# Attention and MLP on one core: another order of a pair's steps, with roundings moved to GpSimd

## The chip, the cores and the metric

The kernel runs on one core of a Trainium2 chip. The metric is the device time of one execution in microseconds (us); smaller is better. The engines are PE (matrix products and transposes), DVE (VectorE), ACT (ScalarE), POOL (GpSimd) and SP, whose queue issues the DMAs. Each engine works through its own queue in the order in which the program was written; engines wait for each other through semaphores.

## What is computed

Attention with a bias that depends on the distance of two positions, then an MLP with an ELU. Everything is float32.

```
B, H, S, D = 4, 8, 576, 64
scores = q @ k^T / sqrt(D) + bias          # bias: 8 heads x 576 x 576, a small net of log1p|i-j| / log1p(i)
attn   = exp(scores - rowmax);  attn /= attn.sum(-1) + 1e-9
x      = (attn @ v) as 2304 tokens x 512
g      = elu(x @ w_in)                     # 512 -> 2048
out    = g @ w_out                         # 2048 -> 512
```

## The kernel before

There are three stages: the bias tables (to about 50 us), attention (to 275 us), and the MLP. The change is in attention and its hand-over to the MLP.

**Pairs.** Attention works on 16 pairs: a pair `n` is two heads (e = 0, 1) of one batch, four pairs a batch. The 576 queries of a pair are four blocks of 128 rows (u = 0..3, two heads each) and a tail of 64 rows, in which both heads share one block (u = 4). For a block the steps are, by the letters used in the lists:

- `S`: scores on PE (line 361), three products of a high and a low part for each half of the keys. A block's two heads take the two score tiles `ps0`, `ps1`; the tail takes one.
- `X`: on DVE, bias added, row minimum of the negated scores (line 388), which frees the score tile; then on ACT the exponential with its row sum (line 400); after head 1 a GpSimd copy `md` of the last 64 key columns of both heads (line 403).
- `T`: transposes on PE of the exponentials into two of three banks `w` (line 474; the tail's, `T4`, at 483 to 487). `M` transposes the `md` tiles: with two digits into spare columns of a score tile (line 458), with one digit into a `w` bank (line 443).
- `P`, `Q`: copies of the transposed tiles from PSUM to the tiles `pta`, `ptb` (lines 495 to 501, and 446, 462). The letter at the end says the engine, A for ACT, V for DVE.
- `V`: products with the values on PE (line 517), half 0 from `pta`, half 1 from `ptb`, five key chunks each. `C` copies the sum out (line 523); there is one bank `v`, so a half's first product waits for the `C` of the half ahead of it.

**Weights.** Between these steps stands the decoding of one of 16 weight tiles a pair, whose raw words come by one 1 MB DMA into a single tile `raw` (line 330): `scale` (POOL, line 335), `low` (DVE, line 339), `sign` (DVE, line 343, after which the next `raw` is loaded), `shift` (DVE, line 345, then an integer add on POOL, line 348), and the store by SP.

**Split of q and k.** `high` rounds the next pair's q and k to fp32r (four casts, line 139), `rest` subtracts (four subtractions on POOL, line 143).

**The lists.** `STEPS` is a table of five lines, written out by hand. A pair's turn runs through the five lines; a step that begins with `a` is of this pair, with `y` of the pair before it, so that the two overlap. `step` walks a line and emits its steps, so the list sets the order on every engine's queue. `FIRST` serves pair 0, `SECOND` pair 1, `LATE` (alike `STEPS`) the last four, `LAST` what is left after pair 15. After each line, `aside` issues loads, the store of a weight tile, and `pad_v`; `flush` issues the attention output's stores. `early` holds work for the MLP, by pair and place: loads of the MLP's input (`load_x`: x and its row factors rr), its scaling (`scale_x`), and the parts of `B11` to `B22` (`high_x`, `low_x`); `one` and `two` in a list are the places for those that run on DVE, in pairs 6, 7, 10 and 12 to 15.

**The sums' inverses.** After each four pairs the row sums are lifted by 1e-9 (POOL, line 415), inverted (DVE, line 411), transposed (`turn`), copied (`turned`) and stored.

Of the kernel before, what the change touches and what calls it, by code (L numbers as in the profile page):

```python
# [10 lines left out]
F32 = mybir.dt.float32  # L11
# [13 lines left out]
def kernel(  # L25
# [517 lines left out]
    PRODS = (("A11", "B11"), ("S2", "T2"), ("A12", "B21"), ("S3", "T3"), ("S1", "T1"), ("A22", "T4"), ("S4", "B22"))  # L543


    def load_x(j, r, h, part=None):
        t0 = (2 * j + h) * HB
        c0 = KH * r
        if not part:
            if h == 0:  # L550
                xr[j, r] = keep.tile([P, KH, 2, HB], F32, tag=f"xr{r}", name=f"xr{r}", bufs=1)
            st["rr", j, r, h] = keep.tile([P, KH, HB], F32, tag="rr", name="rr", bufs=1)
        x, rr = xr[j, r][:, :, h], st["rr", j, r, h]
        M = NCH * P
        done = 0
        while done < HB:
            b, s = divmod(t0 + done, S)
            m = min(HB - done, S - s)
            if part in (None, min(done, 1)):
                nc.sync.dma_start(out=x[:, :, done:done + m], in_=xd[b][:, c0:c0 + KH, s:s + m])  # L560
                rows = rd[b].rearrange("(h u) t -> h (u t)", h=HP)[c0:c0 + KH]
                cuts = [(0, s, m, s)]
                if s < M:
                    cuts.append((1, s, min(m, M - s), M + P + s))
                if s + m > M:
                    k = max(s, M)
# [60 lines left out]
    def attention():  # L627
# [14 lines left out]
        )  # L642
        FIRST = (
            "aS0 aS4 aX00 aX01 high rest aX40",
# [2 lines left out]
            "aS3 aT1 w3 aP10A aX30 aX31",  # L647
            "zS0 aT4 aP11V aP40A aP41A",
        )
        SECOND = (  # L650
            STEPS[0].replace("low ", "").replace("aX00", "aX00 scale").replace("aX01", "aX01 low"),
            *STEPS[1:],
        )
        LATE = (
# [5 lines left out]
        )  # L660
        LAST = (
            "yT2 yP20A yP21V yV00 yV01 yV02 low yM0 yV03 yQ0A",
            "yT3 yP30A yP31V yV04 sign yC0V shift yM1 yQ1A",
            "yV10 yV11 yV12 yV13 yV14 yC1A",
        )
        late = []

        V, G = nc.vector, nc.gpsimd
        early = {
            (5, 0): [(load_x, 0, 0, 0)],  # L670
            (6, "one"): [(scale_x, 0, 0, 0, V)],
            (6, 0): [(load_x, 0, 1, 0)],
            (7, "one"): [(scale_x, 0, 1, 0, V)],
            (8, 0): [(load_x, 0, 0, 1, 0)],
            (9, 0): [(load_x, 0, 0, 1, 1)],
            (10, "one"): [(scale_x, 0, 0, 1, V)],
# [26 lines left out]
        def step(N, line):  # L703
            for tok in line.split():
# [21 lines left out]
                if k == "S":  # L726
# [4 lines left out]
                        ]  # L731
                    if ("ps", n, i[0]) not in st:
                        scores(n, i[0], first_bank if (n, i[0]) == (0, 1) else pair_bank)
                    if i[0] == NCH and n % HP == 0 and n > 0:
                        turn(n // HP - 1, (n, NCH))
                elif k == "X":
                    expo(n, *i)
                    if i[0] == NCH and n % HP == 0 and n > 0:
                        late.extend(turned())
                elif k == "T":  # L740
                    trans_p(n, i[0])
                elif k == "P":
# [31 lines left out]
        def aside(n, i):  # L774
            if i == 4:
                weights(n - 1, "store")
            if i == 0 and n > 0:
                load_v(n)
                pad_v(n - 1)
            if i == 2:  # L780
                if 0 < n < NP - 2:
                    load_pair(n + 2)
            if n == 0 and i == 1:
                open_banks()
            if n > 0 and n % HP == 0:
                if i == 0:
                    lift(n // HP - 1)
                if i == 1:
                    invert(n // HP - 1)
            others(n, i)  # L790
            if n < NP - 1:
                return
            if i == 0:
                load_w(0)
                load_w(1)
            if i == 2:
                high_w(0)
            if i == 3:
                low_w(0, nc.vector)
            if i == 4:  # L800
                load_w(2)

        for n in range(NP):
            for i, line in enumerate(FIRST if n == 0 else SECOND if n == 1 else STEPS if n < NP - 4 else LATE):
                flush()
                step(n, line)
                aside(n, i)
# [371 lines left out]
```

## Time and profile before

| what | value |
| --- | --- |
| time, median of 3 runs | 660.24 us (659.71 to 660.47) |
| the profiled execution: its time | 660.98 us |
| its span | 659.2 us |
| PE busy, share of the span | 650.7 us, 99% |
| DVE, ACT, POOL busy | 477.5, 449.9, 144.3 us |
| chain that ended last, by engine | PE 87%, ACT 6%, DMA 4% |

The span is what the profiler saw between the first and the last instruction; 1.8 us lie around it. A busy share is an average over three stages with different limits; in attention one pair's turn takes about 13.4 us and is read by itself below. PE's starts are recorded and its ends are modelled, so distances from start to start are used for PE.

### The profile page before, as it was taken

How to read it: one execution, taken by the hardware profiler on the slowest of the kernel's cores; microseconds unless marked ns; L12 is line 12 of the kernel's file. 1: busy time of each engine (PE TensorE's matmuls, PEld its weight loads, DVE VectorE, ACT ScalarE, POOL GpSimd, SP SyncE). 2: the span in 40 equal slices, each digit the busy share in tenths (PEclk: the TensorE clock that was granted, in tenths of full speed). 3: DMA queues.
4: the chain of work that ended last, by engine and by line, in shares of the span. 5: the costliest groups of instructions: out<-in, count | busy, mean ns of one | idle time of the engine just before them, and what ended most of it. 6: DMA issues, size and time to landing. Idle time of an engine off the chain costs nothing.

```text
span 659.2 us, 14081 instructions
## 1 busy us (share of the span) xinstructions
PE 650.7 (99%) x5334; PEld 524.5 (80%) x5334; DVE 477.5 (72%) x992; ACT 449.9 (68%) x984; POOL 144.3 (22%) x207
## 2 busy tenths in 40 slices
PE   8999999999999999999999999999999999999997
PEld 5446767767677677799998889899899899899896
DVE  6998888888888998886778998554466554444444
ACT  7998999989999999775666676544345544444443
POOL 1003566655665667600000000000000000000000
PEclk9999999999999999999999999999999999999999
DMA  6998667786877666456798678976854465444102
GB/s 171 221 230 236 213 226 216 200 270 208 243 240 242 192 206 226 145 178 230 254 329 316 241 255 334 382 254 241 284 207 191 198 253 229 191 176 175 65 1 95
DMA packets 47427, 144.42 MB, mean 219 GB/s; under 512 B 9968, under 2 KB 22912, under 8 KB 39680
## 3 DMA queue, kind: packets, MB, share of 16 engines
q1 hardware_dynamic: 45872, 141.01, 64.7%
q10 hardware_dynamic: 1488, 2.52, 1.1%
q8 instruction: 42, 0.69, 0.4%
q14 instruction: 25, 0.20, 0.1%
HBM read 91.92 MB, written 40.97 MB: 202 GB/s over the span
## 4 chain that ended last, share of the span: by engine, by line
PE 87%; ACT 6%; DMA 4%; DVE 1%; issue 1%; SPq 1%; DVEq 0%; ACTq 0%
PE acc L919 30%; PE h L972 27%; PE wv L517 12%; PE ps L361 10%; PE wt L474 5%; ACT rel L241 3%; ACT bo L264 2%; DMA bias<-bo 2%; DMA raw<-in_wd_dram 2%; PE wm L443 1%; DMA T<-in_rtab_dram 1%; PE acc L972 1%; PE wt L483 1%; ACT ss L400 1%; DMA out_dram<-os 0%
## 5 line engine op out<-in xcount | busy, mean ns | idle before, releaser
L919 PE MATMUL acc<-wB,gh 128*128 128x512 f32 x528 | 171.3, 392 | 0.0
L972 PE MATMUL h<-bias 128*128 128x384 f32 x552 | 111.5, 338 | 0.0
L919 PEld LDWEIGHTS acc<-wB,gh 128*128 128x128 f32 x528 | 98.1, 188 | 14.3
L388 DVE CUSTOM_DVE_ANT_0 ss<-ps,bias 128x576 f32<-128x576 f32 x128 | 91.8, 755 | 21.2 <-PE ps L361 11.3
L972 PEld LDWEIGHTS h<-bias 128*128 128x128 f32 x552 | 99.9, 188 | 7.5 <-DVE rs L430 0.4
L919 PE MATMUL acc<-wB,gl 128*128 128x512 f32 x264 | 103.8, 393 | 0.0
L400 ACT ACTIVATE ss<-ss,nm 128x576 f32<-128x576 f32 x128 | 99.3, 779 | 6.4 <-DVE nm L388 6.0
L952 ACT CAST gh<-e 128x384 fp32r<-128x384 f32 x96 | 49.3, 514 | 40.4 <-DVE e L951 39.6
L957 ACT ACTIVATE e<-c 128x384 f32<-128x384 f32 x66 | 34.7, 525 | 53.5 <-DVE c L1003 53.4
L946 DVE TENSOR_TENSOR gl<-e,gh 128x384 fp32r<-128x384 f32 x96 | 53.2, 554 | 19.0 <-ACT gh L952 16.6
L957 ACT ACTIVATE e<-h 128x384 f32<-128x384 f32 x28 | 13.8, 491 | 68.8 <-PE h L972 68.8
L951 DVE SCALAR_TENSOR_TENSOR e<-e,c 128x384 f32<-128x384 f32 x66 | 36.8, 557 | 30.6 <-ACT e L958 30.5
L972 PE MATMUL h<-bias,wA 128*128 128x384 f32 x276 | 56.3, 338 | 0.0
L919 PEld LDWEIGHTS acc<-wB,gl 128*128 128x128 f32 x264 | 49.5, 187 | 7.8
L972 PEld LDWEIGHTS h<-bias,wA 128*128 128x128 f32 x276 | 50.2, 188 | 3.8
L958 ACT ACTIVATE e<-e 128x384 f32<-128x384 f32 x96 | 50.5, 526 | 3.0
L1003 DVE TENSOR_TENSOR c<-h,u 128x384 f32<-128x384 f32 x66 | 36.7, 556 | 20.1 <-PE h L972 20.1
L474 PEld LDWEIGHTS wt<-ident,ss 64*128 64x128 f32 x1024 | 39.2, 139 | 11.7 <-issue 6.9
L251 PE MATMUL bps<-rel,cs 128*32 128x288 f32 x576 | 47.3, 413 | 0.8 <-ACT bo L264 0.4
L361 PE MATMUL ps<-kh,qh 64*128 64x288 f32 x256 | 45.9, 341 | 1.4 <-ACT pta L462 1.4
L403 POOL TENSOR_SCALAR md<-ss 128x128 f32<-128x128 f32 x64 | 21.2, 331 | 116.5 <-ACT ss L400 112.7
L474 PE MATMUL wt<-ident,ss 64*128 64x64 f32 x1024 | 45.8, 227 | 0.8 <-DVE nm L388 0.4
(145 smaller groups left out, 1217.3 us busy)
## 6 DMA issues: line engine op xcount, KB each, us to landing
wB<-wB SPq DMA_DIRECT2D x22, 1024.0 KB, 6.5
raw<-in_wd_dram SPq DMA_DIRECT2D x16, 1024.0 KB, 5.9
bias<-wA SPq DMA_DIRECT2D x9, 1792.0 KB, 8.9
wA<-wA SPq DMA_DIRECT2D x8, 1792.0 KB, 8.6
wa<-wf SPq DMA_DIRECT2D x20, 512.0 KB, 4.8
wA<-bias SPq DMA_DIRECT2D x5, 1792.0 KB, 9.9
wf<-da SPq DMA_DIRECT2D x16, 512.0 KB, 3.5
bias<-bo SPq DMA_DIRECT2D x17, 288.0 KB, 6.5
```

The source lines that it names most:

```text
L251: nc.tensor.matmul(ps[32 * g:32 * g + 32, f, 0:HS], lhsT=W2, rhs=rel[g][:, f * HS:(f + 1) * HS], start=True, stop=True,)
L361: nc.tensor.matmul(ps[:, f, 0:HS], lhsT=(qh, ql)[q][r, u * P:(u + 1) * P] if u < NCH else qd[n % 2][q], rhs=k[r, f * HS:(f + 1) * HS], sta ...
L388: nc.vector.tensor_tensor_reduce(out=s.rearrange("p (f x) -> p f x", f=2), in0=st["ps", n, u][e][:, :, 0:HS], in1=bap.rearrange("p (f x) - ...
L400: nc.scalar.activation(s, s, AF.Exp, bias=nm, scale=-1.0, accum_out=st["sm", b][:, hp, col:col + 1])
L474: nc.tensor.transpose(banks[r][:, x * TAIL:(x + 1) * TAIL], ss[q, c:c + P], ident[q, q])
L517: nc.tensor.matmul(st["pv", n, half][e * D:(e + 1) * D, 0:N], lhsT=l, rhs=r, start=start, stop=stop)
L919: nc.tensor.matmul(acc[j, t], lhsT=x[:, t * P:(t + 1) * P], rhs=w, start=(count[j, t] == 1), stop=(count[j, t] == 6 * NQ),)
L946: nc.vector.tensor_sub(gl, t, gh.bitcast(F32))
L952: nc.scalar.copy(g[i, e][0][:, h * HB:(h + 1) * HB], t)
L957: nc.scalar.activation(t, src, AF.Relu, scale=-1.0)
L958: nc.scalar.activation(t, t, AF.Exp, scale=-1.0)
L972: nc.tensor.matmul(ps, lhsT=a[f][c], rhs=x[y][c], start=(start and k == 0), stop=(stop and k == len(todo) - 1), skip_group_check=not start,)
```

## The change

The table `STEPS` is written anew. The tail's scores stand second (S0, S4, S1, S2, S3) where they stood third; transposes stand behind the values and ahead of a set of scores more often; `low` and `sign` stand around the second exponential, `shift` in the last line. On the copies: the middle half `Q1` goes from DVE to ACT, `C0` and the tail's two copies `P40`, `P41` from ACT to DVE. The roundings `high` become `highG`, on GpSimd. `SECOND` is `STEPS`, so pair 1's `scale` is issued at `low`. Pair 15 has a list of its own (`FINAL`), and `LAST` is in another order. `load_x` can issue x alone or rr alone; the first two loads of x go two pairs and one pair ahead of their rr. `scale_x` of the second goes from pair 7 to pair 8. The transpose of the sums stands behind the third set of scores of a pair, whichever that is; lift and inversion stand behind the first two exponentials.

```
 STEPS = (
-    "aS0 yM0a0 yT3 yQ01A yV02 one low aX00 yQ00A yP30A aX01 yV01 yV03",
-    ...
-    "aS3 aT4 aP11V yV13 aP40A aP41A yV11 aX30 yV12 aX31 yC1A",
+    "aS0 yM0a0 yT3 yV02 yQ00A yQ01A yP31A aX00 yM1",
+    ...
+    "aS3 aP00A shift aP01A aX30 yV10 yV12 yV11 aX31 yC1A aT4 aP41V aP40V",
 )
-SECOND = (STEPS[0].replace("low ", "").replace("aX00", "aX00 scale").replace("aX01", "aX01 low"), *STEPS[1:])
+SECOND = STEPS
+FINAL = (
+    ...
+    "aS2 rest yC0V aT1 one aP10A aX20 aP11V yV14 yV13 aX21 shift aT0 aP00A",
+    "aS3 yV10 aP01A aX30 aT4 yV12 yV11 aP40V aX31 aP41V yC1A",
+)
 early = {
-    (5, 0): [(load_x, 0, 0, 0)],
+    (3, 0): [(load_x, 0, 0, 0, None, "x")],
+    (5, 0): [(load_x, 0, 0, 0, None, "r")],
     (6, "one"): [(scale_x, 0, 0, 0, V)],
-    (6, 0): [(load_x, 0, 1, 0)],
-    (7, "one"): [(scale_x, 0, 1, 0, V)],
+    (6, 0): [(load_x, 0, 1, 0, None, "x")],
+    (7, 0): [(load_x, 0, 1, 0, None, "r")],
+    (8, "one"): [(scale_x, 0, 1, 0, V)],
...
-    if i[0] == NCH and n % HP == 0 and n > 0:
-        turn(n // HP - 1, (n, NCH))
+    if n % HP == 0 and n > 0:
+        st["nth"] = st.get("nth", 0) % (NCH + 1) + 1
+        if st["nth"] == 3:
+            turn(n // HP - 1, (n, i[0]))
...
-    for i, line in enumerate(FIRST if n == 0 else SECOND if n == 1 else STEPS if n < NP - 4 else LATE):
+    for i, line in enumerate(FIRST if n == 0 else SECOND if n == 1 else FINAL if n == NP - 1 else STEPS):
```

On PE, from the spare transposes behind S0 (line 458) on: T3 is line 474, values are line 517, the tail's scores are the rows with `qd`, the other scores those with `qh`. Before:

```order
L458 MATMUL ps<-ident,md 128x64 x4
L474 MATMUL wt<-ident,ss 128x64 x16
L517 MATMUL wv<-pta,vv 64x320 x6
L361 MATMUL ps<-kh,qh 128x288 x2
L361 MATMUL ps<-kl,qh 128x288 x2
L361 MATMUL ps<-kh,ql 128x288 x2
L361 MATMUL ps<-kh,qh 128x288 x2
L361 MATMUL ps<-kl,qh 128x288 x2
L361 MATMUL ps<-kh,ql 128x288 x2
L474 MATMUL wt<-ident,ss 128x64 x16
L517 MATMUL wv<-pta,vv 64x320 x2
```

The same place on PE after the change:

```order
L458 MATMUL ps<-ident,md 128x64 x4
L474 MATMUL wt<-ident,ss 128x64 x16
L517 MATMUL wv<-pta,vv 64x320 x2
L443 MATMUL wm<-ident,md 128x128 x2
L361 MATMUL ps<-kh,qd_108 128x288
L361 MATMUL ps<-kl,qd_108 128x288
L361 MATMUL ps<-kh,qd_109 128x288
L361 MATMUL ps<-kh,qd_108 128x288
L361 MATMUL ps<-kl,qd_108 128x288
L361 MATMUL ps<-kh,qd_109 128x288
L517 MATMUL wv<-pta,vv 64x320 x2
L474 MATMUL wt<-ident,ss 128x64 x16
```

One key chunk of values stands where three stood, the tail's scores follow S0 in place of S1's, and T2 stands behind values (ahead of S1) where it stood behind S1.

On POOL, one pair, from its `vz` (pad of the values' tail) to the next. Before, with `da` the weights' scale (335) and add (348):

```order
L154 TENSOR_SCALAR vz_114<-vv 64x64 x2
L348 TENSOR_TENSOR da<-da,dm 128x1024
L403 TENSOR_SCALAR md<-ss 128x128
L143 TENSOR_TENSOR kl<-kk,kh 128x576
L143 TENSOR_TENSOR ql<-qq,qh 128x512
L143 TENSOR_TENSOR qd_109<-qq,qd_108 64x64 x2
L403 TENSOR_SCALAR md<-ss 128x128 x2
L335 TENSOR_SCALAR da<-raw 128x1024
L403 TENSOR_SCALAR md<-ss 128x128
```

The same engine after the change:

```order
L154 TENSOR_SCALAR vz_114<-vv 64x64 x2
L335 TENSOR_SCALAR da<-raw 128x1024
L403 TENSOR_SCALAR md<-ss 128x128
L139 CAST qd_108<-qq 64x64 x2
L139 CAST qh<-qq 128x512
L139 CAST kh<-kk 128x576
L403 TENSOR_SCALAR md<-ss 128x128
L143 TENSOR_TENSOR kl<-kk,kh 128x576
L143 TENSOR_TENSOR ql<-qq,qh 128x512
L143 TENSOR_TENSOR qd_109<-qq,qd_108 64x64 x2
L403 TENSOR_SCALAR md<-ss 128x128
L348 TENSOR_TENSOR da<-da,dm 128x1024
```

The four casts of line 139 have come in, and the weights' add stands behind the subtractions, near the pair's end.

## Rows read from the trace of the kernel before

**Rows 1.** The page, its first section: busy us, share of span, instructions.
```profile
PE 650.7 (99%) x5334; PEld 524.5 (80%) x5334; DVE 477.5 (72%) x992; ACT 449.9 (68%) x984; POOL 144.3 (22%) x207
```

**Rows 2.** Busy time by stretch, a pair with `one` in it (pair 10).
```profile
core 0: us, PE busy (x) PEld busy (x) DVE busy (x) ACT busy (x) POOL busy (x), PEclk, DMA share, GB/s
185.50:199.00 13.50, 13.50 (x178) 9.71 (x176) 11.93 (x31) 12.72 (x36) 8.56 (x13) 1.00 0.73 228
```

**Rows 3.** Timeline of DVE: tail reduces of pairs 6, 7, 14, 15 (start, length).
```profile
139.81 0.76 DVE L388 CUSTOM_DVE_ANT_0 st<-ps,biast 128x576 f32<-128x576 f32 x1 [0.36 <-PE ps L361]
153.18 0.76 DVE L388 CUSTOM_DVE_ANT_0 st<-ps,biast 128x576 f32<-128x576 f32 x1 [0.36 <-PE ps L361]
...
247.29 0.76 DVE L388 CUSTOM_DVE_ANT_0 st<-ps,biast 128x576 f32<-128x576 f32 x1 [0.37 <-PE ps L361]
260.74 0.76 DVE L388 CUSTOM_DVE_ANT_0 st<-ps,biast 128x576 f32<-128x576 f32 x1 [0.37 <-PE ps L361]
```

**Rows 4.** Timeline of PE inside pair 10: start, length, line, count.
```profile
187.46 0.80 PE L474 MATMUL wt<-ident,ss 64*128 64x64 f32 x16
...
189.96 0.40 PE L361 MATMUL ps<-kh,qh 64*128 64x288 f32 x2
...
190.72 0.30 PE L361 MATMUL ps<-kh,ql 64*128 64x288 f32 x2
190.85 0.66 PE L474 MATMUL wt<-ident,ss 64*128 64x64 f32 x16
191.44 0.76 PE L517 MATMUL wv<-pta,vv 128*64 128x320 f32 x4
...
193.07 0.29 PE L361 MATMUL ps<-kh,qd 128*128 128x288 f32 x1
193.29 0.76 PE L517 MATMUL wv<-pta,vz 128*64 128x320 f32 x4
193.98 0.71 PE L474 MATMUL wt<-ident,ss 64*128 64x64 f32 x16
194.50 0.38 PE L361 MATMUL ps<-kh,qh 64*128 64x288 f32 x2
...
195.41 0.71 PE L474 MATMUL wt<-ident,ss 64*128 64x64 f32 x16
```

**Rows 5.** Pairs 5 and 6: the chain that ended last, then DVE's and PE's timeline.
```profile
123.90 9.97 DMA raw<-in_wd_dram
133.90 0.69 DVE L339 TENSOR_SCALAR dm<-raw 128x1024 int32<-128x1024 uint32 x1 [1.73 <-DMA raw<-in_wd_dram]
136.37 0.40 PE L361 MATMUL ps<-kh,qh 64*128 64x288 f32 x2 [1.41 <-ACT pta L462]
```

**Rows 6.** POOL's groups, whole span: busy us, mean ns of one, idle before.
```profile
L348 POOL TENSOR_TENSOR da<-da,dm 128x1024 int32<-128x1024 int32 x16 | 42.1, 2634 | 3.8 <-DVE da L345 2.5
L143 POOL TENSOR_TENSOR kl<-kk,kh 128x576 fp32r<-128x576 f32 x15 | 21.3, 1418 | 11.9 <-DVE kh L139 9.1 <-DMA kk<-in_k_dram 1.9 <-DMA raw<-in_wd_dram 0.8
L335 POOL TENSOR_SCALAR da<-raw 128x1024 f32<-128x1024 f32 x16 | 19.1, 1192 | 1.0 <-DMA raw<-in_wd_dram 0.9
L143 POOL TENSOR_TENSOR qd<-qq,qd 64x64 fp32r<-64x64 f32 x30 | 9.5, 317 | 1.1
L194 POOL COPY pick<-ident 128x128 f32<-128x128 f32 x1 | 0.3, 291 | 0.1
```

**Rows 7.** Hand-over to the MLP, timelines of POOL and DVE.
```profile
274.49 6.37 POOL L348 TENSOR_TENSOR da<-da,dm 128x1024 int32<-128x1024 int32 x1 [2.54 <-DVE da L345]
...
277.66 0.95 DVE L591 TENSOR_TENSOR T<-xr,xr 128x768 f32<-128x768 f32 x1
278.99 2.69 DVE L591 TENSOR_TENSOR T<-xr,T 128x768 f32<-128x768 f32 x1
```

**Rows 8.** DVE's and ACT's groups in pair 8; last a timeline row of DVE.
```profile
L343 DVE SCALAR_TENSOR_TENSOR dm<-raw,dm 128x1024 uint32<-128x1024 uint32 x1 | 1.2, 1220 | 0.0
L339 DVE TENSOR_SCALAR dm<-raw 128x1024 int32<-128x1024 uint32 x1 | 0.7, 690 | 0.0
L500 ACT COPY pta<-wt 128x256 f32<-128x256 f32 x2 | 0.7, 370 | 0.0
253.56 0.95 DVE L603 TENSOR_TENSOR bias<-xr,bias 128x768 fp32r<-128x768 f32 x1
```

More of the change, by code (lines that the diff above doesn't have):

```diff
@@ L543, with load_x @@
     PRODS = (("A11", "B11"), ("S2", "T2"), ("A12", "B21"), ("S3", "T3"), ("S1", "T1"), ("A22", "T4"), ("S4", "B22"))
-    def load_x(j, r, h, part=None):
+    def load_x(j, r, h, part=None, what="xr"):
         t0 = (2 * j + h) * HB
@@ L549, in load_x @@
         if not part:
-            if h == 0:
+            if h == 0 and "x" in what:
                 xr[j, r] = keep.tile([P, KH, 2, HB], F32, tag=f"xr{r}", name=f"xr{r}", bufs=1)
-            st["rr", j, r, h] = keep.tile([P, KH, HB], F32, tag="rr", name="rr", bufs=1)
-        x, rr = xr[j, r][:, :, h], st["rr", j, r, h]
+            if "r" in what:
+                st["rr", j, r, h] = keep.tile([P, KH, HB], F32, tag="rr", name="rr", bufs=1)
+        x, rr = xr[j, r][:, :, h], st.get(("rr", j, r, h))
         M = NCH * P
@@ L558, in load_x @@
             m = min(HB - done, S - s)
-            if part in (None, min(done, 1)):
+            if part in (None, min(done, 1)) and "x" in what:
                 nc.sync.dma_start(out=x[:, :, done:done + m], in_=xd[b][:, c0:c0 + KH, s:s + m])
+            if part in (None, min(done, 1)) and "r" in what:
                 rows = rd[b].rearrange("(h u) t -> h (u t)", h=HP)[c0:c0 + KH]
@@ L649, in attention @@
         )
-        SECOND = (
-            STEPS[0].replace("low ", "").replace("aX00", "aX00 scale").replace("aX01", "aX01 low"),
-            *STEPS[1:],
-        )
-        LATE = (
[5 rows of a table removed]
+        SECOND = STEPS
+        LATE = (
[5 rows of a table added]
+        )
+        FINAL = (
[5 rows of a table added]
         )
         LAST = (
-            "yT2 yP20A yP21V yV00 yV01 yV02 low yM0 yV03 yQ0A",
-            "yT3 yP30A yP31V yV04 sign yC0V shift yM1 yQ1A",
-            "yV10 yV11 yV12 yV13 yV14 yC1A",
+            "low yT2 yV00 yV01 yM0 yP21A yP20V yT3",
+            "yV02 yQ0A yP30A yV04 yV03 yP31A sign yV11 yM1 yC0V",
+            "yV13 yV12 shift yQ1A yV14 yV10 yC1A",
         )
@@ L733, in step @@
                         scores(n, i[0], first_bank if (n, i[0]) == (0, 1) else pair_bank)
-                    if i[0] == NCH and n % HP == 0 and n > 0:
-                        turn(n // HP - 1, (n, NCH))
+                    if n % HP == 0 and n > 0:
+                        st["nth"] = st.get("nth", 0) % (NCH + 1) + 1
+                        if st["nth"] == 3:
+                            turn(n // HP - 1, (n, i[0]))
                 elif k == "X":
                     expo(n, *i)
-                    if i[0] == NCH and n % HP == 0 and n > 0:
-                        late.extend(turned())
+                    if n % HP == 0 and n > 0:
+                        if i == [0, 0]:
+                            lift(n // HP - 1)
+                        if i == [0, 1]:
+                            invert(n // HP - 1)
+                        if "wr" in st and st["wr"][1] == (n, i[0]):
+                            late.extend(turned())
                 elif k == "T":
@@ L784, in aside @@
                 open_banks()
[L785 to L789, printed above, removed]
             others(n, i)
```

19 rows, old and new, of tables (FINAL, LATE, STEPS) are left out of this document.

## The prediction

> **What bounds the kernel now.** I read the page first: PE is busy for 99% of the span [rows 1], so the question is whether that busy time is work or only a modelled end. The busy time by stretch says for one pair in attention: PE 13.50 of 13.50 us, ACT 12.72, DVE 11.93, POOL 8.56 [rows 2]. ACT is near its limit too, so either could set the pace. The tail reduces give the pace: 13.37 us from pair 6 to pair 7 and 13.45 from pair 14 to 15 [rows 3]; the pairs from 12 on, which also carry work for the MLP, are the slower ones.
>
> PE's timeline inside pair 10 decides it [rows 4]. If PE waited for ACT or DVE, gaps between groups would differ from pair to pair. They repeat, and they follow the kind of neighbour: a set of 16 transposes starts values 0.59 us after its own start when it follows scores (190.85 to 191.44), and starts scores 0.52 us after its own start behind values (193.98 to 194.50). I see two places only where transposes run longer than their 0.66: T3 takes 0.80 and T1 0.71. T3 needs the second exponential of block 3, which on ACT stands behind the copies of the tail; that is a wait. So PE bounds attention before the change, with some 0.2 us a pair of real waiting. The MLP is a chain of PE instructions on both sides and isn't touched.
>
> One place stands out. In pair 6 the DVE waits 1.73 us for `raw` and PE then stands still for 1.41 us [rows 5]. That weight tile was asked for in pair 5 and landed 9.97 us later, since the load of x with its rr was issued just ahead of it on SP.
>
> **The change part by part.**
>
> *PE's order.* No product or transpose is added or dropped, so only the neighbours change. Scores followed by values start them 0.22 us after their last product (193.07 to 193.29), scores followed by transposes 0.13 (190.72 to 190.85) [rows 4]. S1 and S3 now have values behind them: +0.09 twice, +0.18. T2 and T4 stand ahead of scores in place of values: 0.52 for 0.59, -0.07 twice, -0.14. The copies of the tail leave ACT, so T3's wait should go: -0.14; T1's -0.05 likewise. The sum is -0.15 a pair. The bounds are 0 (both waits come back as others) and -0.3 (a set of scores behind transposes also starts quicker, which these rows don't settle). Pairs 1 to 5, 7, 9 and 11 have nothing else: 8 x -0.15 = -1.2 us.
>
> *Tail second.* S4 needs one score tile, so its products run while DVE still reduces block 0's second head. The ring of score tile, reduce, next scores gets shorter by about one tail's turn. As PE is the bound this buys slack and no time; I cost it at nothing, and what it must cover is the next point.
>
> *Copies between ACT and DVE.* The tail's copies are two of 0.37 us [rows 8] and two smaller ones; with C0 they go to DVE, and Q1 comes to ACT. DVE loses the four casts and gains these, about even. ACT gets about 1 us of air (an estimate: the two of 0.37, as much again for the smaller ones and C0, less Q1). Queued behind the tail's copies on DVE is the next pair's first reduce, and behind that S4 and S1; the copies fit into the time in which DVE would wait for S0's products, so nothing, with +0.3 a pair if they don't fit.
>
> *Roundings on GpSimd.* The trace has no cast on POOL. The nearest rows are the one-input copies: 291 ns for 128 columns and 1192 for 1024 [rows 6], about 1.0 ns a column. That makes 0.74 us for k (576), 0.68 for q (512) and 0.23 for each small one: 1.9 us a pair. From the other side, the subtractions have two inputs and the same fp32r output: 1418 for 576, 317 for 64, thus 3.3 us for the four. I take 1.9, since a cast has one input and the fp32r output costs a subtraction nothing that its rate shows. POOL then has 8.56 + 1.9 = 10.5 us of work a pair of 13.2.
>
> POOL and DVE also shut each other out. At the hand-over the integer add took 6.37 us, where the fifteen others average 2.38 ((42.1 - 6.37) / 15), while DVE ran two-input instructions, and the second of DVE's two subtractions took 2.69 for 0.95, as it ended only after that add [rows 6, 7]. DVE has three such instructions a pair, `low` and `shift` of 0.69 and `sign` of 1.22 [rows 8]: 2.6 us. Then 10.5 + 2.6 = 13.1 of 13.2 us. That is full, but not over, and POOL's results have most of a pair before they are wanted; what costs is DVE waiting for the POOL instruction that runs. `sign` stands ahead of S1's reduces and `shift` ahead of S3's, each with a cast or a subtraction of up to 1.4 us in its way, and the ring's new slack must cover that. In plain pairs I think it does: nothing, bounds 0 to +0.5 a pair.
>
> The Trainium skill, SBUF — State Buffer, section Who interferes with whom, says that DVE with two SBUF inputs or in a two-port mode and GpSimd share one port pair, and that the later of the two blocks fully for the other's whole instruction. The trace agrees, 6.37 for 2.38 us. By that rule it speaks against this change; what it would give here is the first rival below.
>
> *`one` and `two` behind the second block.* In pairs 6, 8 and 10 a scaling of 0.95 us (the same form as L603) [rows 8] stands ahead of C0 on DVE, and C0 must end before the first product of half 1. In pairs 12 to 14 a cast of 768 columns comes on top, an estimate of 0.5 from the 0.69 of 1024. POOL's casts run just then. For 6, 8 and 10 I take 0 (bounds -0.15 and +0.65); for 12 to 14 I take +0.3 each, +0.9 (bounds 0 and +1.05), as C0 ends late by about one POOL cast less the slack.
>
> *Loads.* x goes in pair 3, rr in pair 5, so SP reaches the next `raw` sooner and one long transfer is out of its way. On the other side `raw` is asked for only after the later `sign`. I take the whole 1.4 us; bounds 0 and 1.4.
>
> *Sums' transposes, `FINAL`, `LAST`.* The transpose and its small copy stand behind the third scores and have the same neighbours in kind: nothing. At the end PE has one run of values fewer in `LAST` and one more, split by T4, in `FINAL`: nothing, bounds -0.5 and +1.
>
> **Sum.** -1.2 + 0.9 - 1.4 = -1.7 us. Against the profiled execution's 660.98 that makes 659.3; its span, 659.2, would go to 657.5. The median of the runs is 660.24, so 658.5.
>
> **Rivals.**
>
> *The shared port decides (slower).* If POOL's work and DVE's exclusive instructions simply add up in one pair, a plain pair is at 13.1, a pair with `one` at 14.0 and a pair with both at 14.5 us. Then pairs 6, 8 and 10 lose 0.65 each and 12 to 14 about 1.05 each: -1.2 - 1.4 + 1.9 + 3.2 = +2.5, so 662.7. It decides as soon as the sum passes 13.2, and only 0.1 is left there. For it: the add at the hand-over [rows 7], and POOL near full. Against it: POOL can run late without anyone waiting.
>
> *Casts at the two-input rate (much slower).* POOL's 3.3 for 1.9 us gives 14.5 a pair, over the pace in each of the 14 pairs that round for the next: 14 x 1.1 - 1.4 = +14, so 674. Against it: the copy of 128 columns at 291 ns.
>
> *Nothing moves.* PE was the bound and stays it; the waits of T3 and T1 turn into others, and the late `raw` waits in another pair, since it is asked for later. That gives 659.9 at -0.3.
>
> *All of it works.* -0.25 in 14 pairs, -1.4, and pairs 12 to 14 at the pace of the rest (13.45 to 13.37, -0.1 each): -5.2, so 655.0.
>
> **How the numbers follow.** The forecast has 0.45, the shared port 0.22, nothing moves 0.15, all of it 0.10, slow casts 0.08. A measurement of this kernel can tell about 0.2% from no change, 1.3 us. The forecast lies just past that, so I split it 0.37 faster and 0.08 same; all of it is faster; nothing moves is 0.03 faster and 0.12 same; the shared port is 0.06 same and 0.16 slower; slow casts are slower. Faster 0.50, same 0.26, slower 0.24. The range takes in all of it at 654.5 and the shared port at 662.7 with some margin, 663.5, and leaves the slow casts out.
>
> **What would show it.** Right: tail reduces 13.2 us apart in pairs 2 to 5, no wait for `raw` in pair 6, casts of about 0.7 us on POOL, T3 at 0.66. The shared port: `sign`, `shift` or `one` longer than 1.22, 0.69 and 0.95, and PE idle ahead of half 1's values, released by C0. Slow casts: 1.3 us and more in POOL's groups. Wrong altogether would be a plain pair slower than 13.37 with PE waiting for reduces, for then the ring is the bound and not PE.

## The result, and the profile after

The changed kernel takes 663.76 us (median of 8 runs, 663.48 to 667.63), the kernel before 660.38 on the same chip. The ratio is 1.0061, 95% interval 1.0048 to 1.0075: slower by 0.6%. The forecast was 658.5 us, in a range of 654.5 to 663.5.

The profiled execution took 663.5 us with a span of 661.7, against 660.98 and 659.2 before: 2.5 us more in the traces. First the page's first section (busy us, share, instructions), which answers [rows 1]:

```profile
PE 652.1 (99%) x5334; PEld 523.7 (79%) x5334; DVE 488.3 (74%) x995; ACT 437.3 (66%) x925; POOL 186.8 (28%) x263
```

POOL has 42.5 us more. The busy time of the stretch that answers [rows 2], pair 10 again:

```profile
core 0: us, PE busy (x) PEld busy (x) DVE busy (x) ACT busy (x) POOL busy (x), PEclk, DMA share, GB/s
185.20:198.70 13.50, 13.50 (x180) 9.62 (x178) 12.82 (x29) 11.72 (x29) 11.74 (x17) 1.00 0.57 155
```

ACT and DVE have changed places as the second busiest engine, and PE has no gap in either.

To place the 2.5 us, I take as a pair's start the first spare transpose behind S0 (PE, line 458), which stands at the same place in all the lists, and as the end's length the stretch from pair 15's start to the MLP's first product. In us:

| stretch | before | after | e_rr | e_pad_wa | e_all | e_beforeL |
| --- | --- | --- | --- | --- | --- | --- |
| pair 1 | 14.09 | 14.71 | 14.21 | 14.20 | 14.13 | 14.01 |
| pairs 2, 3, 5, 7, mean | 13.36 | 13.24 | 13.23 | 13.24 | 13.23 | 13.36 |
| pairs 4 and 8, mean | 13.49 | 13.53 | 13.56 | 13.55 | 13.54 | 13.50 |
| pair 6 | 14.85 | 13.24 | 13.25 | 13.25 | 13.25 | 13.37 |
| pair 9 | 13.36 | 14.42 | 13.20 | 14.52 | 13.23 | 13.38 |
| pair 11 | 13.37 | 13.34 | 13.26 | 13.27 | 13.68 | 13.37 |
| pairs 12 to 14, sum | 40.70 | 41.01 | 40.99 | 40.99 | 40.82 | 40.68 |
| end | 20.16 | 22.79 | 22.75 | 20.89 | 20.83 | 20.18 |

The columns with an e_ are experiments, below. From before to after: the late `raw` of pair 6 is gone (-1.61) and the plain pairs 2, 3, 5 and 7 are 0.12 shorter (pairs 4 and 8, which also transpose sums, are not), but pair 9 has 1.06 more, pair 1 0.62, pairs 12 to 14 0.31, and the end 2.63. The rows that show the three large losses follow.

**Pair 9.** SP's, then DVE's timeline (start, length, what; in brackets the idle time before it and what ended it):

```profile
162.26 0.43 SPq L561 DMA_DIRECT2D xr<-xd  x1
166.98 1.92 SPq L572 DMA_DIRECT2D rr<-rd  x3
169.00 0.54 SPq L330 DMA_DIRECT2D raw<-in_wd_dram  x1
...
165.83 1.12 DVE L579 TENSOR_TENSOR xr<-xr,rr 128x768 f32<-128x768 f32 x1
175.54 0.70 DVE L339 TENSOR_SCALAR dm<-raw 128x1024 int32<-128x1024 uint32 x1 [1.52 <-DMA raw<-in_wd_dram]
```

SP stands still from 162.7 to 166.98 with the load of rr at its head. There is one rr tile, and DVE's scaling, which reads the old rr, ends only at 166.95. The next `raw` is queued behind that load and lands at 175.5, where DVE waits 1.52 us for it.

The same happens once more two pairs later, with the load of (10, 0) ahead of the scaling at `one` of pair 10. SP's, then DVE's timeline:

```profile
189.90 0.45 SPq L561 DMA_DIRECT2D xr<-xd  x1
194.50 1.92 SPq L572 DMA_DIRECT2D rr<-rd  x3
196.52 0.54 SPq L330 DMA_DIRECT2D raw<-in_wd_dram  x1
...
202.12 0.70 DVE L339 TENSOR_SCALAR dm<-raw 128x1024 int32<-128x1024 uint32 x1 [0.39 <-DMA raw<-in_wd_dram]
```

SP stands still from 190.35 to 194.50. Here the transfer comes less late, and pair 11 takes 13.34 us, 0.1 more than the plain pairs.

**The end.** POOL's, ACT's, DVE's and PE's timelines in pair 15 and the closing lists:

```profile
262.85 1.05 ACT L612 CAST bias<-wa 128x1024 fp32r<-128x1024 f32 x1 [0.59 <-DMA wa<-wf]
264.43 0.65 PE L474 MATMUL wt<-ident,ss 64*128 64x64 f32 x14 [0.34 <-ACT pta L495]
...
266.58 2.37 POOL L348 TENSOR_TENSOR da<-da,dm 128x1024 int32<-128x1024 int32 x1
268.89 0.70 DVE L339 TENSOR_SCALAR dm<-raw 128x1024 int32<-128x1024 uint32 x1
268.90 2.36 POOL L593 TENSOR_TENSOR xr<-xr,xr 128x768 f32<-128x768 f32 x1
...
271.89 1.51 POOL L154 TENSOR_SCALAR vz<-vv 64x64 f32<-64x64 f32 x2
...
272.18 0.75 PE L517 MATMUL wv<-pta,vz 128*64 128x320 f32 x2 [0.41 <-POOL vz L154]
273.45 0.48 PE L517 MATMUL wv<-pta,vz 128*64 128x320 f32 x1 [0.52 <-POOL vz L154]
```

The new order reaches the rounding of the MLP's first weights sooner, before their transfer `wa` has landed, and a copy behind it on ACT makes PE wait. Then the product with `vz` stands early in the closing lists, while `vz` is still behind the integer add and a sum in POOL's queue.

**Pair 1.** A row of the chain that ended last:

```profile
62.25 4.97 DMA bias<-bo
```

And one of ACT's timeline:

```profile
67.56 0.59 ACT L495 COPY ptb<-wt 128x512 f32<-128x512 f32 x1 [1.16 <-DMA kk<-in_k_dram]
```

This is P31A, the first write of `ptb` in the program, now ahead of the exponential X00. The chain puts its wait down to the last transfer of the bias tables, which ends at 67.2; ACT's row names the load of kk, so which of the two it was isn't settled.

### The profile page after: what moved, and what is told of

Its sections match the earlier page's. It is cut to its first block, busy times and chain, and to the rows that moved or that the text cites. A ratio compares the mean times of both kernels' runs of the same rounds, so it can differ in the third digit from the quotient of the medians.

```text
span 661.7 us, 14040 instructions
## 1 busy us (share of the span) xinstructions
PE 652.1 (99%) x5334; PEld 523.7 (79%) x5334; DVE 488.3 (74%) x995; ACT 437.3 (66%) x925; POOL 186.8 (28%) x263
## 4 chain that ended last, share of the span: by engine, by line
PE 85%; DVE 6%; issue 3%; DMA 3%; SPq 1%; POOL 1%; ACT 1%; DVEq 0%; ACTq 0%; POOLq 0%
PE acc L929 30%; PE h L982 27%; PE wv L517 11%; PE ps L361 8%; PE wt L474 4%; DVE rel L243 3%; PE bps L251 1%; DMA raw<-in_wd_dram 1%; DMA wa<-wf 1%; PE wm L443 1%; PE wt L483 1%; DMA bias<-bo 1%; PE unread L186 1%; DVE ss L388 1%; PE acc L982 1%
## 5 line engine op out<-in xcount | busy, mean ns | idle before, releaser
L388 DVE CUSTOM_DVE_ANT_0 ss<-ps,bias 128x576 f32<-128x576 f32 x128 | 92.9, 751 | 12.3 <-PE ps L361 8.8
L403 POOL TENSOR_SCALAR md<-ss 128x128 f32<-128x128 f32 x64 | 31.7, 495 | 84.1 <-ACT ss L400 81.5
L361 PE MATMUL ps<-kh,qh 64*128 64x288 f32 x256 | 48.3, 337 | 0.6 <-DVE nm L388 0.6
L517 PE MATMUL wv<-pta,vv 128*64 128x320 f32 x256 | 47.9, 451 | 0.0
```

The lines of the kernel that those rows point to most:

```text
L361: nc.tensor.matmul(ps[:, f, 0:HS], lhsT=(qh, ql)[q][r, u * P:(u + 1) * P] if u < NCH else qd[n % 2][q], rhs=k[r, f * HS:(f + 1) * HS], sta ...
L388: nc.vector.tensor_tensor_reduce(out=s.rearrange("p (f x) -> p f x", f=2), in0=st["ps", n, u][e][:, :, 0:HS], in1=bap.rearrange("p (f x) - ...
L517: nc.tensor.matmul(st["pv", n, half][e * D:(e + 1) * D, 0:N], lhsT=l, rhs=r, start=start, stop=stop)
```

## The experiments

All are compared with the kernel before on the same chip. Read from it: the kernel after is +0.61%. Ratio and interval are formed from the runs of both kernels, so they can differ from the quotient of the two medians by up to 0.1%.

| run | median us | ratio to before, 95% interval |
| --- | --- | --- |
| e_oldend | 662.68 | 1.0033 (1.0021 to 1.0045) |
| e_oldend2 | 662.85 | 1.0047 (1.0032 to 1.0061) |
| e_pad | 662.66 | 1.0038 (1.0024 to 1.0052) |
| e_pad_wa | 661.79 | 1.0029 (1.0018 to 1.0040) |
| e_rr | 661.89 | 1.0026 (1.0016 to 1.0036) |
| e_p31 | 663.29 | 1.0047 (1.0035 to 1.0059) |
| e_best | 661.57 | 1.0020 (1.0011 to 1.0030) |
| e_best_V | 673.47 | 1.0199 (1.0186 to 1.0211) |
| e_all | 659.88 | 1.0002 (0.9988 to 1.0016) |
| e_all2 | 661.18 | 1.0011 (1.0003 to 1.0020) |
| e_all3 | 660.33 | 0.9997 (0.9988 to 1.0006) |
| e_all4 | 663.74 | 1.0039 (1.0027 to 1.0052) |
| e_beforeG | 660.14 | 0.9993 (0.9983 to 1.0002) |
| e_beforeL | 659.88 | 0.9992 (0.9982 to 1.0002) |
| e_beforeLG | 660.26 | 0.9986 (0.9977 to 0.9994) |

My theory was that the order lost the time at a few places of its own, whatever engine does the roundings. The rival was the one of the prediction: GpSimd's load and the port that it shares with DVE.

**e_rr: the load of (8, 0) behind `one`.**

```
-            (8, 0): [(load_x, 0, 0, 1, 0)],
+            (8, 2): [(load_x, 0, 0, 1, 0)],
```

> The kernel after, with the load of a quarter of x and of its reciprocals, (8, 0), moved behind line 2 of pair 8, that is behind scale_x at place one, whose buffer rr it takes. Theory A: SP does not stand still for 4.6 us behind line 0, the raw transfer of pair 8 lands before its use at 174 us, the period from pair 9 to pair 10 falls from 14.42 to about 13.3 us: 663.8 - 1.1 = 662.7 us (662.4 to 663.0). Theory B (the raw wait travels with the load, as it went from pair 6 to pair 9): another pair of 9 to 11 takes 0.5 to 1.2 us more, 663.4 to 664.0 us.

SP's rows at the place where after has its wait:

```profile
163.75 0.33 SPq L330 DMA_DIRECT2D raw<-in_wd_dram  x1
...
167.21 0.59 SPq L561 DMA_DIRECT2D xr<-xd  x1
167.90 2.15 SPq L572 DMA_DIRECT2D rr<-rd  x3
...
165.30 1.11 DVE L579 TENSOR_TENSOR xr<-xr,rr 128x768 f32<-128x768 f32 x1
173.42 0.73 DVE L339 TENSOR_SCALAR dm<-raw 128x1024 int32<-128x1024 uint32 x1
```

`raw` is asked for 5.25 us sooner (0.5 of it from pair 1), DVE doesn't wait for it, and pair 9 takes 13.20 us. Theory A came true by its mechanism. The median fell by 1.9 us, more than the 1.2 that pair 9 gives; pair 1 takes 0.5 less in this trace, which the edit doesn't touch (see e_p31).

**e_pad and e_pad_wa: the two late transfers of the end.**

```
+            if i == 1:
+                pad_v(NP - 1)
...
-        pad_v(NP - 1)
```

> The kernel after, with one call moved: pad_v of pair 15, the GpSimd copy of 1.5 us on which the value products of the tail wait, is issued behind line 1 of pair 15 instead of behind its last line. Theory A: the product found it 2 us late because it stands behind the lift's products and the T1 and T3 sums in GpSimd's queue; with it ahead of them the two PE waits of 0.4 and 0.5 us and the weight-load wait of 2.1 us on vz are gone, but the late wa transfer (0.6 us) stays: 663.8 - 1.7 = 662.1 us (661.6 to 662.8). Theory B (GpSimd as a whole is late): what moves ahead pushes the sums of T1 and T3 back, and something else of that queue is waited for: 663.4 to 664.0 us.

The waits for `vz` went, and the end stayed at 22.75 us. The median, 662.66, lies in theory A's range, but the trace shows theory B's outcome: other waits came in their place, and most of the 0.6 us by which its span is shorter than after's is pair 1 (14.32 for 14.71). The timelines of ACT, PE, POOL and DVE in e_pad:

```profile
262.75 1.05 ACT L612 CAST bias<-wa 128x1024 fp32r<-128x1024 f32 x1 [1.09 <-DMA wa<-wf]
264.34 0.65 PE L474 MATMUL wt<-ident,ss 64*128 64x64 f32 x14 [0.83 <-ACT pta L495]
...
268.50 1.81 POOL L593 TENSOR_TENSOR xr<-xr,xr 128x768 f32<-128x768 f32 x1
268.81 2.05 DVE L339 TENSOR_SCALAR dm<-raw 128x1024 int32<-128x1024 uint32 x1
271.63 0.71 PE L474 MATMUL wt<-ident,ss 64*128 64x64 f32 x15 [1.20 <-DVE ptb L495]
```

The same two instructions stand in the rows of after at 268.89 and 268.90, and there DVE was first by 0.01 us: DVE took its 0.70, POOL 2.36. Here POOL was first by 0.3 us: POOL took its own 1.81, DVE 2.05 for 0.70, and a copy behind it on DVE made PE wait 1.20 us. So at this place the shared port costs PE time in the trace in which POOL came first.

In e_pad_wa the first `wa` load is issued behind line 2 of pair 14 as well:

```
+            if n == NP - 2 and i == 2:
+                load_w(0)
...
-                load_w(0)
                 load_w(1)
```

> The kernel after with two things earlier: pad_v of pair 15 behind line 1 of pair 15, and the first load of the MLP's weights, wa, behind line 2 of pair 14 rather than behind line 0 of pair 15. With pad_v alone PE's waits for vz went and two others came: 0.83 us for a copy on ACT that stood behind the rounding of wa (ACT waited 1.09 us for its transfer), and 1.20 us for a copy on DVE that stood behind low's first step, which took 2.05 us instead of 0.70 beside GpSimd's T3 sum. Theory A (each wait is its own, and taking one away leaves the next late step): the first is gone, the second stays: 662.7 - 0.8 = 661.9 us (661.5 to 662.4). Theory B (all hang on GpSimd): what ACT gains PE loses at the second wait, which grows to 2 us: 662.5 to 662.9 us.

Now ACT doesn't wait for `wa`, and DVE's step came first again, at 268.39 against POOL's 268.41. The end took 20.89 us, 1.9 less than after, with no PE wait for `vz`, `wa` or that copy. The median, 661.79, is as theory A said, but only half by its reasons: the second wait didn't stay, since DVE won the port.

**e_oldend, e_oldend2, e_best: the lists of before for the end.** In the first, `FINAL` and `LAST` are those of before; the second also makes pair 14's last copies on ACT; the third is the second with e_rr's edit.

```
 FINAL = (
-    "aS0 yM0a0 yT3 yV02 yQ00A yQ01A yP31A aX00 yM1", ...
+    "aS0 yM0a0 yT3 yQ01A yV02 one low aX00 yQ00A yP30A aX01 yV01 yV03", ...
 )
+JOINT = (*STEPS[:4], STEPS[4].replace("aP41V aP40V", "aP40A aP41A"))
```

> The kernel after, with the list of pair 15 and the closing lists of the kernel before (its FINAL and LAST lists taken back). Theory A (the time was lost at three places of the order, most of it, 2.6 us, behind the first step of pair 15): the stretch from pair 15's first step to the first matmul of the MLP falls from 22.8 us back to about 20.2 us, so 663.8 - 2.6 = 661.2 us (660.8 to 661.6). Theory B (GpSimd, loaded by the roundings, is what makes the end late, whatever list stands there): the stretch stays above 22 us, 663.3 to 663.9 us.

> As the run with the lists of before in pair 15 and behind it, and with the last two copies of pair 14, P40 and P41, on ACT as those lists take for granted (in the first run DVE still made the four copies of the tail, 0.42 + 0.23 us twice, as pair 15 began, a load step of 1.32 us stood behind them, and PE waited 1.48 us for the exponential). Theory A (the order of pair 15 and of the closing lists is the loss): the joint's wait is gone, from pair 15's first step to the end of the program it takes 404.5 us as before, rather than 407.0 in the kernel after: 663.8 - 2.5 = 661.3 us, less up to 0.5 us if pair 1 finds its transfer early (660.7 to 661.5). Theory B (GpSimd's queue, fuller by the roundings, holds the end whatever the order): 405.5 us or more, 662.2 us or more.

> The kernel after with the two losses taken out together: the load of (8, 0) behind the scale_x whose buffer it takes, and the lists of before for pair 15 and the closing part, joined on ACT. Theory A: the new list is worth what the prediction gave it where it stands alone (13.25 us a plain pair against 13.36, no late raw transfer in pair 6), and the sum is 660.1 - 2.0 in pairs 1 to 14 and 0 in the end: 658.1 us (657.6 to 658.8), faster than before. Theory B (GpSimd's load turns up as a wait elsewhere): 659.8 us or more.

The ends took 21.8, 21.7 and 21.95 us: 0.8 to 1.1 of the 2.63 us came back, and all three runs missed theory A's numbers. The lists don't join where pair 14's last line meets pair 15's first. POOL, DVE and PE in e_best, at pair 15's start, and the tail's reduce of pair 15:

```profile
251.30 2.38 POOL L348 TENSOR_TENSOR da<-da,dm 128x1024 int32<-128x1024 int32 x1
251.66 2.84 DVE L605 TENSOR_TENSOR bias<-xr,bias 128x768 fp32r<-128x768 f32 x1
...
256.97 0.40 PE L361 MATMUL ps<-kh,qh 64*128 64x288 f32 x2 [1.09 <-ACT pta L462]
...
260.41 0.76 DVE L388 CUSTOM_DVE_ANT_0 st<-ps,biast 128x576 f32<-128x576 f32 x1 [0.36 <-PE ps L361]
```

In the new list `shift` stands in the last line, so POOL's add falls into the next pair's line 0, where the old list has `one`: DVE's subtraction of 0.95 us lasts 2.84. I had blamed DVE's copies for the joint (e_oldend); with these on ACT it was there still. What the end of before takes by itself can still be read behind the joint: from the tail's reduce of pair 15 to the MLP's first product it is 14.18 us in e_best (260.41 to 274.59) and 14.18 in before (260.74 to 274.92). So the old closing lists cost no more here than there, and what these ends have over 20.16 us is lost ahead of that reduce. The last two runs came out at theory B's numbers, and the port is its reason, though at the joint and not by the roundings. In its plain pairs e_best has what the prediction gave the list, 13.24 us, and there is no late `raw` in pair 6.

**e_best_V: the roundings back on DVE.** e_best, with `high` for `highG`:

> The kernel of the run beside it (both losses taken out) with one word changed: the roundings highG back on VectorE, at the same place of the list. Theory A (the roundings on GpSimd cost PE nothing; they free 1.27 us a pair of a DVE that is busy nearly without a gap in the new list): DVE takes 4 x 0.445, 4 x 0.412 and 8 x 0.206 us in four pairs more and gets back what shift and qd lost to the lock, 0.6 to 0.7 us a pair: the pairs take up to 0.6 us more, 13 pairs: 658.1 to 666 us, and not faster than the run beside it. Theory B (the port that DVE and GpSimd share is what costs): 0.5 us or more faster than the run beside it.

It is 11.9 us slower, more than either theory had. Busy time from 80 to 250 us in e_best:

```profile
80.00:250.00 170.00, 169.39 (x2213) 120.13 (x2209) 157.04 (x358) 149.59 (x369) 148.51 (x209) 1.00 0.73 228
```

The same stretch in e_best_V:

```profile
80.00:250.00 170.00, 164.63 (x2090) 115.55 (x2088) 159.82 (x385) 140.61 (x349) 116.07 (x148) 1.00 0.69 215
```

PE has gaps of 5.4 us instead of 0.6, 4.1 of them in 13 waits for DVE's reduces, and a plain pair takes 13.9 us. DVE's busy share times the mean of pairs 2 to 14 (13.36 us in e_best, 14.20 here) is an estimate of its work in a pair: 12.3 us without the roundings and 13.4 with them, all that e_best's mean pair holds. So it isn't their move that the change loses by; the new list depends on it.

**e_beforeG, e_beforeL, e_beforeLG: one part alone.** The kernel before with `highG`, with the new table of loads, with both:

> The kernel before with one word changed in each list: highG for high, the roundings on GpSimd, at their old place behind two in the third line. Theory A (the roundings on GpSimd cost PE nothing where the order leaves GpSimd the time, and DVE, with 8 us idle in four pairs there, has no use for the 1.27 us a pair): 660.2 us (659.8 to 660.8). Theory B (GpSimd's 1.73 us a pair and its hold on the port stand in the way of DVE): 0.2 us a pair or more, 662.5 us or more.

> The kernel before with the change's table of loads and nothing else: x of two quarters loaded two pairs earlier than its reciprocals, scale_x of the second quarter a pair later. In the lists of before place one stands in line 0, ahead of the load of (8, 0), so no buffer is waited for. Theory A (the load part was right: it takes away the late raw transfer of pair 6, 1.5 us, and only its meeting with the new place of one made a new one): 660.2 - 1.5 = 658.7 us (658.3 to 659.2), faster than both kernels. Theory B (the late transfer turns up in another pair in any list): 659.8 us or more.

> The kernel before with the new loads and with highG for high. Theory A (each part alone took 0 to 0.7 us off; together they add): pair 6 at 13.4 us, pairs 12 to 14 at 13.5, 13.4 and 13.4 instead of 13.8, 13.5 and 13.5: 659.9 - 0.5 = 659.4 us (659.0 to 659.8). Theory B (nothing left to win, the bound of the old list is PE): 659.9 us or more.

The roundings on GpSimd change nothing in the old list that the runs can tell, as theory A says; in its trace pairs 12 to 14 take 40.23 us, 0.47 less than in before, and pair 6 has 0.13 more. With the loads pair 6 falls from 14.85 to 13.37 us and no other pair rises by more than 0.02, but the median falls by 0.7 us only, not 1.5, and its interval reaches to no change. Theory A's 658.7 didn't come, and the time is at theory B's number though no other pair got longer.

Both together give a ratio of 0.9986 (0.9977 to 0.9994): of the sixteen kernels compared here the only one whose interval lies below before, by 0.9 us of the ratio and 0.6 of the medians, with pair 6 at 13.40 and pairs 12 to 14 at 40.27 us. The expected 659.4 stood on e_beforeL's 659.88, where before took 660.56, and so meant 1.2 us below before; what came is half to four fifths of that.

**e_p31: P31A behind X00 in pair 1.**

> The kernel after, with one step of pair 1 moved: the copy P31A behind the exponential X00 rather than ahead of it. Theory A: P31A is the first write of ptb, whose room the bias phase's last transfer (landed at 67.2 us) still reads; X00 is then no longer held up behind that wait of 1.16 us on ACT, the period of pair 1 falls from 14.71 to about 14.1 us: 663.8 - 0.6 = 663.2 us (662.9 to 663.5). Theory B: the wait goes to what stands behind P31A now (M1's bank, P30A and T2), and pair 1 keeps its 14.7 us: 663.6 to 664.0 us.

The time, 663.29, and pair 1 at 14.21 us are as theory A has them. But e_rr, e_pad and e_oldend, with pair 1 untouched, have 14.16 to 14.32, and all traces of the new list with pair 1 as in after (e_best_V apart) 14.13 to 14.80. ACT's row in e_rr:

```profile
67.00 0.59 ACT L495 COPY ptb<-wt 128x512 f32<-128x512 f32 x1 [0.66 <-DMA kk<-in_k_dram]
```

The copy's wait is half a microsecond shorter there, and pair 1 goes with that wait: 0.57 us and 14.13 in e_all, 0.66 and 14.21 in e_rr, 1.16 and 14.71 in after, 1.22 and 14.80 in e_all3. What ends it sooner or later, the bias tables' last transfer or another, isn't shown: the chain of after and e_all3 runs through that transfer, that of e_rr doesn't. Two traces with the edit, this one and e_all2's with 14.22 us, don't show that the edit helps: inconclusive.

**e_all, and three attempts to better it.** e_all is the kernel after with e_rr's and e_pad_wa's moves. e_all2 adds e_p31's, and yC0 of pair 15 on ACT; e_all3 is e_all with yC0 on ACT in pairs 4, 8 and 12; e_all4 is e_all3 with `one` of pair 15 moved into the fifth line.

> The kernel after with its three misplaced steps moved and nothing else: the load of (8, 0) behind line 2 of pair 8, pad_v of pair 15 behind its line 1, the first wa load behind line 2 of pair 14. Theory A (these waits are separate and their prices add): 663.8 - 1.2 - 1.9 = 660.7 us (660.0 to 661.2); in the profile the pairs take what they take with the first step alone (188.2 us for pairs 1 to 14) and the end 20.9 us. Theory B (a wait goes, another comes): 661.5 us or more.

> The run beside it with two copies more: in pair 1 P31A behind the exponential X00, and in pair 15 the copy of V0 (yC0) on ACT instead of DVE, whose reduces PE waits for there twice by 0.35 us. Theory A (what the end still has over before, 0.7 us, is DVE's queue): up to 0.7 us less in the end and 0.0 to 0.5 in pair 1: 660.0 us (659.4 to 660.7). Theory B (ACT, which also carries the exponentials, takes over as the late engine): no less than the run beside it.

> The run with the three steps moved (659.9 us), and in pairs 4, 8 and 12 the copy yC0 on ACT, as in the lists of before, instead of DVE. Theory A (in these pairs PE waits 0.2 us for DVE's copy of V0, because the turn's reciprocal and copy stand in DVE's queue too): the three waits on xs are gone, pairs 4, 8 and 12 take 13.4, 13.4 and 13.8 us instead of 13.5, 13.5 and 13.9: 659.9 - 0.4 = 659.5 us (659.2 to 659.8). Theory B (ACT is then late for an exponential): 659.9 us or more.

> The run beside it, and in pair 15 place one (a step of 0.95 us on DVE) moved from the fourth line behind aT1 to the fifth behind yV12. Theory A (the 0.7 us that the end still has over before is PE waiting twice for DVE's reduces behind that step): the end takes 20.3 to 20.6 us instead of 20.8, 659.2 us (658.8 to 659.5). Theory B (what is left is the end's order on PE and its other copies): no less than the run beside it.

With three steps moved the kernel is level with before: 3.9 us came back, more than the parts' 1.2 and 1.9; in the trace pair 1 gives 0.6 of it. One loss of the same kind as pair 9's was left in, since no run moved the load of (10, 0). DVE's row in pair 11 of e_all:

```profile
200.57 0.69 DVE L339 TENSOR_SCALAR dm<-raw 128x1024 int32<-128x1024 uint32 x1 [0.72 <-DMA raw<-in_wd_dram]
```

Pair 11 takes 13.68 us there, 0.45 more than the plain pairs; over the traces of the new list (e_best_V apart) it varies between 13.25 and 13.68. What moving it would give the median wasn't run.

The others show why the end is delicate. In e_all2 POOL's sum came to the port first (266.76 against DVE's 267.18), and PE waited 1.1 us as in e_pad; the copy of V0, now on ACT, made it wait 0.7 more. In e_all3 pairs 4 and 8 still take 13.55 and 13.53 us: the copy of V0 wasn't what they lose by. PE's rows in pair 8 of after show most of it, the transpose of the sums (line 424):

```profile
163.73 0.29 PE L361 MATMUL ps<-kh,ql 64*128 64x288 f32 x2
163.95 0.29 PE L424 MATMUL ps<-ident,sm 128*36 128x128 f32 x1
164.17 0.76 PE L517 MATMUL wv<-pta,vv 128*64 128x320 f32 x4
```

Without it values start 0.22 us after the last product of these scores (150.49 to 150.71 in pair 7), with it 0.44: 0.22 of the 0.29 us that pair 8 has over pair 7. In before, where it stands behind the tail's scores, it adds 0.11.

In e_all4, POOL, DVE and PE:

```profile
264.90 2.35 POOL L348 TENSOR_TENSOR da<-da,dm 128x1024 int32<-128x1024 int32 x1
265.37 2.70 DVE L605 TENSOR_TENSOR bias<-xr,bias 128x768 fp32r<-128x768 f32 x1
...
268.68 0.68 PE L474 MATMUL wt<-ident,ss 64*128 64x64 f32 x15 [2.31 <-DVE pta L501]
```

Moved by one line, the step `one` meets POOL's add, lasts 2.70 us instead of 0.95, and PE pays 2.31. Theory A was wrong there; theory B's number came, no less than the run beside it, but not by its reason. The 0.7 us that the end of e_all has over before is therefore not explained.

## Why the prediction was wrong

**PE's order: the sum right in a plain pair, in part by luck.** I said -0.15; pairs 2, 3, 5 and 7 measure -0.10 to -0.14. PE's rows in pair 10 of after, which answer [rows 4]:

```profile
190.43 0.71 PE L474 MATMUL wt<-ident,ss 64*128 64x64 f32 x16
190.95 0.38 PE L361 MATMUL ps<-kh,qh 64*128 64x288 f32 x2
...
191.69 0.30 PE L361 MATMUL ps<-kh,ql 64*128 64x288 f32 x2
191.92 0.76 PE L517 MATMUL wv<-pta,vv 128*64 128x320 f32 x4
```

Transposes still start scores after 0.52 us, scores start values after 0.23. That PE bounds a pair held: PE stands still nowhere in pair 10. But the terms came out otherwise. In the mean of pairs 2, 3, 5 and 7, T3 with the spare transposes, to the first values, went from 0.84 to 0.80 us: -0.03 where I took -0.14 for a wait, and T3 isn't at 0.66, one of my signs. (In [rows 4] the set at 193.98 is 0.71 long too, which I passed over: that length alone doesn't tell of a wait.) The scores, which were to cost +0.18, cost +0.09. T1 gave 0.06, T2 and T4 0.13, as forecast. Two errors cancelled. And only four of the eight pairs that I multiplied by took what a plain pair takes: pair 4 is 0.05 longer, since the transpose of the sums has no like neighbours (I had priced it at nothing), pair 11 gave 0.03, and pairs 1 and 9 lost. The eight together measure +1.2 us for -1.2.

**Tail second, and the copies: right.** The tail's reduce came 0.36 us after DVE was free [rows 3] and now comes with no wait ahead of it:

```profile
122.17 0.76 DVE L388 CUSTOM_DVE_ANT_0 st<-ps,biast 128x576 f32<-128x576 f32 x1
135.40 0.76 DVE L388 CUSTOM_DVE_ANT_0 st<-ps,biast 128x576 f32<-128x576 f32 x1
```

These are pairs 5 and 6, 13.23 us apart. The slack covers `sign` and `shift`.

**Roundings on GpSimd: the price was right, the port half right.** POOL's groups over the span, which answer [rows 6]:

```profile
L348 POOL TENSOR_TENSOR da<-da,dm 128x1024 int32<-128x1024 int32 x16 | 39.9, 2496 | 2.1 <-DVE da L345 2.1
L143 POOL TENSOR_TENSOR qd<-qq,qd 64x64 fp32r<-64x64 f32 x30 | 15.8, 527 | 1.1
L139 POOL CAST kh<-kk 128x576 fp32r<-128x576 f32 x14 | 9.3, 661 | 0.0
L139 POOL CAST qh<-qq 128x512 fp32r<-128x512 f32 x14 | 8.5, 607 | 0.0
L139 POOL CAST qd<-qq 64x64 fp32r<-64x64 f32 x28 | 6.5, 232 | 1.7
```

661 + 607 + 2 x 232 ns make 1.73 us a pair, where I took 1.9. The lock is there: the small subtraction takes 527 ns for 317, and in pairs 7 to 10 `shift` 1330 for 685. In plain pairs nobody waits for that, as I said; the first rival's 0.65 us in pairs 6, 8 and 10 didn't come (13.24, 13.53 and 13.26 us, where pair 8 had 13.49 before). The time fell a microsecond above that rival's 662.7 us, and still it wasn't its mechanism: its signs came, but small. Besides the longer `shift`, `one` took 1.11 us for 0.95 in pair 12, and PE waits for C0 ahead of half 1's values in pairs 12 to 14 alone, by 0.29, 0.16 and 0.16 us, most of it the work of `one` and `two` themselves. But in the experiments with moved steps the port decides whether PE waits some 1.1 to 2.3 us at the joint or in the end.

By the rule of the Trainium skill, SBUF — State Buffer, section Who interferes with whom, the later of the two engines is blocked for the other's whole instruction. The rows at 268.5 to 268.9 us agree on both sides to about 0.15 us, 2.36 us for POOL's 1.81 where it came second and 2.05 for DVE's 0.70 where DVE did.

**`one` and `two`: the price came in pairs 12 to 14, but not as a loss against before,** and **what their move does to SP was left out.** PE's row ahead of half 1's values in pair 12 of after:

```profile
222.43 0.65 PE L517 MATMUL wv<-ptb,vz 128*64 128x256 f32 x4 [0.29 <-DVE xs L523]
```

C0 (line 523) ends late, as I said. The transposes ahead of these values take 1.04, 0.81 and 0.81 us in the three pairs, against 0.59 in a plain one: +0.89 for +0.9. The three pairs lost only 0.31 against before, since they gain by PE's order too and before had its own losses there, 40.70 us for three plain pairs' 40.08. I priced `one` behind the second block by what stands behind it on DVE. But `scale_x` at `one` also gives the only rr tile back, and the load that waits for it stands behind line 0 on SP. In before `one` is in line 0 and comes first. That made +1.06 us in pair 9, shown by e_rr, and up to 0.45 in pair 11.

**Loads: -1.4 was the trace's value, not the runs'.** The wait in pair 6 went, by 1.61 us in the trace; but the loads alone take 0.7 us off the median (e_beforeL; by the interval between 1.2 less and 0.1 more). Pair 6 has the wait in both traces with the old loads, of before (14.85 us) and of e_beforeG (14.98), so why the medians differ by less is open.

**`FINAL`, `LAST`: the term that decided.** "Nothing, bounds -0.5 and +1" was reached by counting runs of values on PE. It measured +2.63, and without this term alone the kernel after would be level with before in the traces. I didn't ask what POOL has in its queue when the closing lists want `vz`, nor when `wa` lands against the step that rounds it. e_pad_wa shows that these make 1.9 of the 2.63; the other 0.7 stays open.

**Pair 1** was counted among the plain ones. It took 0.04 to 0.71 more than in before in those traces of the new list that leave it as it is in after (e_best_V apart), by how long the first write of `ptb` waits.

In the traces: -0.41 in pairs 2 to 5, 7 and 8, -0.14 in 10 and 11, -1.61 in 6, +1.06 in 9, +0.31 in 12 to 14, +0.62 in 1, +0.06 ahead of it, +2.63 in the end: +2.5 us. The gains, 2.2 us, came near the 2.6 forecast, though not pair by pair; pairs 9 and 1 and the end, which I had priced as plain or at nothing, gave 4.3 back.

## What to carry to other kernels

When a step is moved, ask which buffer it gives back as well as which data it makes, and look up on the other queues who waits for that buffer and what is queued behind the waiting one. Price the first and the last turn of a loop by their own queues, since there transfers and side work meet that a turn in the middle never sees. When a cause is found, look for its other places in the same table: the stall of pair 9 stood in pair 10 as well. A wait in one profiled execution is worth what the medians say when it is gone, and a total near a rival's number doesn't prove the rival, nor does a sum that comes out prove its terms.

## What was unexpected of the hardware

Which engine comes to the shared port first changed between kernels with the same lists by a third of a microsecond: DVE ahead by 0.01 us lost nothing (0.70 us), POOL ahead by 0.31 us cost DVE 1.35 (2.05 us) and PE 1.20 behind it. The same DVE subtraction took 0.95, 2.70 and 2.84 us by where POOL's add fell. A one-input rounding on GpSimd cost about 1.15 to 1.19 ns a column (661 ns for 576, 607 for 512), half of what the two-input subtraction into the same type takes (1414 for 576).
